# The first load of a one-token decode layer, w_mod, issued as two DMAs: 16 rows, then 112

## The chip, the cores and the metric

The kernel runs on one core of one Trainium2 chip. A core has five instruction engines (TensorE for matrix products, VectorE, ScalarE, GpSimd and SyncE, which here only issues loads) and 16 DMA engines that move data between the chip's large memory and the core's on-chip buffer of 128 partitions. The metric is the device time of one execution in microseconds, as a median over runs.

## The reference, cut to what matters

One token passes through an attention block over a long cache and a gated feed-forward block. A conditioning vector `c` gives six vectors of 640 numbers that scale and shift the layer norms and gate both blocks:

```python
x = A_x
mod = (_silu(c) @ w_mod).reshape(c.shape[0], 6, 1, -1)   # w_mod: 640 x 3840, bf16
sa, ca, ga, sb, cb, gb = (mod[:, 0], ..., mod[:, 5])
h = _layernorm(x) * (1 + ca) + sa
x = x + ga * _A_ref(h, A_k_cache, A_v_cache, A_wq, A_wo)   # 32 heads, 16384 cached keys and values of 128
h = _layernorm(x) * (1 + cb) + sb
x = x + gb * _B_ref(h, B_w_gate, B_w_up, B_w_down)         # silu(h @ w_gate) * (h @ w_up) @ w_down, 1728 wide
```

The two caches are 32 x 16384 x 128 numbers of two bytes each, 134 MB apiece; all weights together are some 22 MB. Every byte is used once.

## The kernel before, in words

All instructions are recorded first as operations with their dependencies, and a small planner then writes each engine's list in the order of recording, with a wait on a semaphore wherever an operation needs one of another engine (`_Plan.emit`, from line 122). A DMA raises the semaphore of its own channel by 16 when it has landed; a waiter waits for the count that the channel has after the DMA it depends on. Every large load is issued by SyncE, so SyncE's list is the order of the stream of loads, and a load that has to wait (for a buffer to come free) holds back every load behind it. The method that issues a load has line 90, so all loads show as L90.

The stream goes: `w_mod` (line 351), `A_wq` (352), the keys of head pair 0 in two halves, the keys of pair 1, the values of pair 0, and then keys and values of the 16 head pairs by turns, then `A_wo`, `B_w_gate`, `B_w_up`, `B_w_down`. Two loads of 1.2 KB, `c` and `A_x`, are issued by ScalarE at the start (354 and 355). The keys have a ring of two buffers, `kring`, and the values one, `vbuf`. `w_mod` is put into the second key buffer and `A_wq` into the value buffer, since both are free at the start.

The loads are laid out so that every partition takes one piece of the source: partition p of `w_mod` holds rows 5p to 5p+4 of the matrix, 5 x 3840 numbers that lie side by side in memory, 38,400 bytes. A row of the load, in this text, is these 38,400 bytes of one partition. A row of `A_wq` is 40,960 bytes, and a row of one pair's keys or values 65,536 bytes (32,768 in the halves of pair 0).

The start of the kernel runs so: `c` and `x` are turned into columns on TensorE (line 378), ScalarE and VectorE compute the silu of `c` and the layer norm of `x`, and when `w_mod` has landed TensorE multiplies (line 438, 40 matmuls in two halves), VectorE picks the diagonal out (446, 451) and makes `h_col` (460). When `A_wq` has landed, TensorE computes the queries (477) and ScalarE spreads them (484). The load of the keys of pair 1 waits for the second half of the `w_mod` product, because it overwrites the buffer of `w_mod`; the load of the values of pair 0 waits for the last query product. From there on VectorE works through the keys of each pair (a product with the query and two or three folding additions, lines 554, 559, 564 in the loop and 570, 576 for the first and last pair), TensorE sums what is left (544, 584), ScalarE takes the exponential, and TensorE multiplies with the values (518). The keys of pair p+1 are loaded when pair p-1 has been summed.

After the last pair come the output projection with `A_wo` (687, 699), the second layer norm, the gate and up products (724), the down product (771) and two small stores.

The lines around the change are these:

```python
wm_v = kb[:, 0:KC * 6 * D].rearrange("p (k n) -> p k n", k=KC)
wm_src = w_mod.rearrange("(p k) n -> p k n", p=128)
d_wm = dma(wm_v, wm_src, "wm", name="dma_wmod")
d_wq = dma(wq_v, wq_src, "wq", name="dma_wq")
```

`d_wm` is used in one place, as a dependency of the two halves of the product with `w_mod`:

```python
o_mod = [op(PE, lambda e, h=h: f_mod(e, h), deps=[d_wm, o_sc], name="mod_mm%d" % h) for h in range(2)]
```

Of the kernel before, what the change touches and what calls it, by code (L numbers as in the profile page):

```python
# [37 lines left out]
class _Plan:  # L38
# [44 lines left out]
    def dma(self, out_ap, in_ap, key, deps=(), name="", eng="sp", noncontig=False):  # L83
        nc = self.nc

        def fn(e, out_ap=out_ap, in_ap=in_ap, noncontig=noncontig):
            if noncontig:
                with nc.allow_non_contiguous_dma(reason="tiny vector layout change"):
                    return e.dma_start(out_ap, in_ap)
            return e.dma_start(out_ap, in_ap)  # L90

        return self.op(eng, fn, deps, name, chan=self.dma_chan(key))
# [126 lines left out]
def build(nc, A_x, A_k, A_v, A_wq, A_wo, B_wg, B_wu, B_wd, c_in, w_mod, out):  # L219
# [23 lines left out]
    with es:  # L243
        block = es.enter_context(nc.Block())
        plan = _Plan(nc, es)
        op, dma = plan.op, plan.dma
# [10 lines left out]
        wm_v = kb[:, 0:KC * 6 * D].rearrange("p (k n) -> p k n", k=KC)  # L257
# [88 lines left out]
        wm_src = w_mod.rearrange("(p k) n -> p k n", p=128)  # L346
# [1 line left out]
        k_src = lambda p: A_k[0, 2 * p:2 * p + 2].rearrange("h (q t) d -> (h q) t d", q=64)  # L348
        v_src = lambda p: A_v[0, 2 * p:2 * p + 2].rearrange("h (q t) d -> (h q) t d", q=64)

        d_wm = dma(wm_v, wm_src, "wm", name="dma_wmod")
        d_wq = dma(wq_v, wq_src, "wq", name="dma_wq")
        op(ACT, lambda e: e.preload_act_table_set("natural_log_exp_and_others"), name="tbl")
        d_c = dma(rows[:, 0, :], c_in, "c", name="dma_c", eng="act")
# [430 lines left out]
def bass_adaLN_cond__gqa_block_cached__swiglu_ffn__decode_kernel(  # L785
    nc: bass.Bass,
    A_x: bass.AP,
    A_k_cache: bass.AP,
    A_v_cache: bass.AP,
    A_wq: bass.AP,  # L790
    A_wo: bass.AP,
    B_x: bass.AP,
    B_w_gate: bass.AP,
    B_w_up: bass.AP,
    B_w_down: bass.AP,
    c: bass.AP,
    w_mod: bass.AP,
    out: bass.AP,
):
    build(nc, A_x, A_k_cache, A_v_cache, A_wq, A_wo, B_w_gate, B_w_up, B_w_down, c, w_mod, out)  # L800
# [28 lines left out]
```

## Time and profile before

| what | value |
|---|---|
| median of 3 runs | 680.17 us (679.9 to 680.23) |
| profiled execution, its own time | 679.98 us |
| its span from the first to the last instruction | 678.2 us |
| busy: TensorE, VectorE, ScalarE | 366.2, 513.0, 46.7 us (54%, 76%, 7% of the span) |
| DMA | 6355 packets, 290.58 MB, mean 428 GB/s over the span |

The profiled execution's time is 1.78 us longer than its span; the difference lies before the first and after the last instruction. Busy time is the sum over an engine's instructions, so an engine that is busy for 76% of the span may still have waited at every step. The chain of waits is read backwards from the last instruction: at each step it names what released it. The start of an instruction and its duration stand in front of each line of the timeline and of the chain. A DMA issue has two times: the short one for which SyncE (SPq) or ScalarE (ACTq) was occupied in issuing it, and the time from issue to landing, which includes waiting behind earlier loads in the same stream.

### The profile page before, as it was taken

Reading aid. Unit: us, or ns where it says so; the run is one execution under the profiler, and the core shown is the slowest. Engines: PE = TensorE matmul, PEld = TensorE weight load, DVE = VectorE, ACT = ScalarE, POOL = GpSimd, SP = SyncE. Lnnn points to the kernel's source line nnn. Section 1 sums busy time; section 2 is a strip of 40 time slices with the busy share of each in tenths; the row PEclk is TensorE's granted clock in tenths of the full one; section 3 lists DMA queues with packets and bytes.
Section 4 is the critical chain, followed back from the end, with each engine's and each line's share of the span. In section 5 each row is a group of like instructions: output and inputs, shape, how many; then the busy total and the mean of one; then the engine's idle time right before and its main releaser. Section 6 shows DMA issues by size and latency. Waiting matters only on the chain.

```text
span 678.2 us, 5410 instructions
## 1 busy us (share of the span) xinstructions
PE 366.2 (54%) x2068; PEld 146.5 (22%) x2069; DVE 513.0 (76%) x185; ACT 46.7 (7%) x147; POOL 0.7 (0%) x6
## 2 busy tenths in 40 slices
PE   2522275755728274664818375572818465471677
PEld 1111122221312122221302122121212222130236
DVE  2189997959596896959597795959699695959812
ACT  1120000100000000000000010000000000000011
POOL 0000000000000000000000000000000000000000
PEclk9675565655657565565757555575756556575765
DMA  9999999999999999999999999999999999999997
GB/s 372 442 459 433 433 433 430 433 430 433 437 430 433 433 433 433 433 437 433 433 433 433 437 433 433 433 433 433 433 433 433 433 433 433 433 437 433 434 402 305
DMA packets 6355, 290.58 MB, mean 428 GB/s; under 512 B 714, under 2 KB 972, under 8 KB 1484
## 3 DMA queue, kind: packets, MB, share of 16 engines
q1 hardware_dynamic: 6340, 290.48, 99.2%
q8 instruction: 5, 0.08, 0.0%
q10 hardware_dynamic: 8, 0.00, 0.0%
q14 instruction: 2, 0.02, 0.0%
HBM read 290.47 MB, written 0.00 MB: 428 GB/s over the span
## 4 chain that ended last, share of the span: by engine, by line
DMA 48%; DVE 28%; issue 13%; PE 11%; DVEq 0%; ACT 0%; SPq 0%
DMA kring<-in_A_k_cache_dram 45%; DVE kring L554 10%; PE psb L544 7%; DVE kring L559 6%; DVE kring L570 4%; DVE kring L576 3%; DMA vbuf<-in_A_wo_dram 3%; DVE kring L564 3%; PE psb L518 1%; PE psb L724 1%; PE psb L687 1%; PE psb L584 1%; PE psb L699 0%; PE psb L771 0%; DVE pm L590 0%
## 5 line engine op out<-in xcount | busy, mean ns | idle before, releaser
L554 DVE TENSOR_TENSOR kring<-kring,qbc 128x16384 bf16<-128x16384 bf16 x28 | 243.2, 8687 | 96.2 <-DMA kring<-in_A_k_cache_dram 96.2
L544 PE MATMUL psb<-kring,ident 128*128 x448 | 197.5, 607 | 119.3 <-DVE kring L564 119.3
L559 DVE TENSOR_TENSOR kring<-kring 128x8192 bf16<-128x8192 bf16 x28 | 123.8, 4420 | 0.5
L544 PEld LDWEIGHTS psb<-kring,ident 128*128 128x128 bf16 x448 | 53.9, 120 | 247.1 <-issue 246.0
L518 PE MATMUL psb<-vbuf,PZ 128*8 128x512 bf16 x960 | 82.6, 520 | 0.0
L594 PE MATMUL psb<-d,bd_f 128*128 128x64 f32 x32 | 11.0, 446 | 122.0 <-ACT d L592 122.0
L564 DVE TENSOR_TENSOR kring<-kring 128x4096 bf16<-128x4096 bf16 x28 | 64.0, 2286 | 0.5
L570 DVE TENSOR_TENSOR kring<-kring,qbc 128x16384 bf16<-128x16384 bf16 x4 | 34.8, 8688 | 23.4 <-DMA kring<-in_A_k_cache_dram 23.4
L518 PEld LDWEIGHTS psb<-vbuf,PZ 128*8 128x8 bf16 x960 | 27.0, 109 | 60.2 <-issue 51.5
L584 PE MATMUL psb<-kring,ident 128*128 128x128 bf16 x64 | 14.5, 392 | 40.3 <-DVE kring L576 40.3
L594 PEld LDWEIGHTS psb<-d,bd_f 128*128 128x128 f32 x32 | 8.0, 311 | 124.1 <-DVE pm L590 114.4
L576 DVE TENSOR_TENSOR kring<-kring 128x8192 bf16<-128x8192 bf16 (+2 forms) x12 | 31.7, 2645 | 0.3
L533 PEld LDWEIGHTS psb<-sel,acc_sb 128*128 128x128 f32 x128 | 28.5, 311 | 8.4 <-issue 4.3
L533 PE MATMUL psb<-sel,acc_sb 128*128 128x2 f32 x128 | 25.6, 322 | 1.4 <-ACT acc_sb L524 1.4
L524 ACT ACTIVATE acc_sb<-psb 128x512 f32<-128x512 f32 x16 | 9.6, 597 | 212.0 <-PE psb L518 212.0
L602 ACT ACTIVATE PZ<-psb,nb 64x256 bf16<-64x256 f32 x32 | 15.0, 469 | 64.8 <-DVE nb L598 64.6
L584 PEld LDWEIGHTS psb<-kring,ident 128*128 128x128 bf16 x64 | 7.4, 122 | 46.7 <-DVE kring L576 41.6
L592 ACT ACTIVATE d<-negid,pm 128x64 f32<-128x64 f32 x16 | 5.6, 348 | 153.9 <-DVE pm L590 153.9
L477 PE MATMUL psb<-vbuf,h_col 128*128 128x512 bf16 x39 | 11.2, 461 | 8.3 <-DMA vbuf<-in_A_wq_dram 8.3
L537 ACT ACTIVATE OT_sb<-psb 128x2 f32 (+1 forms) x16 | 2.8, 172 | 151.3 <-PE psb L533 151.3
L590 DVE TENSOR_REDUCE pm<-psb 128x1 f32<-128x256 f32 x16 | 6.7, 418 | 3.7 <-PE psb L584 3.7
L477 PEld LDWEIGHTS psb<-vbuf,h_col 128*128 128x128 bf16 x40 | 4.3, 116 | 15.6 <-DMA vbuf<-in_A_wq_dram 8.8
(104 smaller groups left out, 80.4 us busy)
## 6 DMA issues: line engine op xcount, KB each, us to landing
kring<-in_A_k_cache_dram SPq DMA_DIRECT2D x2, 4096.0 KB, 40.3
vbuf<-in_A_wq_dram SPq DMA_DIRECT2D x1, 5120.0 KB, 25.9
kring<-in_w_mod_dram SPq DMA_DIRECT2D x1, 4800.0 KB, 14.2
vbuf<-in_A_wo_dram SPq DMA_DIRECT2D x1, 4480.0 KB, 23.0
kring<-in_B_w_gate_dram SPq DMA_DIRECT2D x1, 2160.0 KB, 18.7
kring<-in_B_w_up_dram SPq DMA_DIRECT2D x1, 2160.0 KB, 23.5
kring<-in_B_w_down_dram SPq DMA_DIRECT2D x3, 640.0 KB, 25.7
vbuf<-in_A_wo_dram SPq DMA_DIRECT2D x1, 640.0 KB, 24.2
```

The costliest lines, as they stand in the source:

```text
L477: last = e.matmul(q_ps[b][:, 0:512], lhsT=h_col[:, k:k + 1].broadcast_to([128, 128]), rhs=wq_v[:, k, g * 512:(g + 1) * 512], start=(k == 0 ...
L518: last = e.matmul(acc_ps[32 * s:32 * s + 8, :], lhsT=PZ[:, j, :], rhs=v_at(p)[:, 4 * j:4 * j + 4, :].rearrange("p t d -> p (t d)"), start= ...
L533: last = e.matmul(OT_ps[:, 0:2], lhsT=acc_sb[:, 128 * i:128 * (i + 1)], rhs=sel[:, i:8:4], start=(i == 0), stop=(i == 3))
L544: last = e.matmul(S_ps[:, 0:T2], lhsT=ident[:], rhs=kring[:, bass.ds(plan.slot(p), 1), :, d].rearrange("p o t -> p (o t)"), start=(d == 0) ...
L554: return e.tensor_tensor(out=kv4, in0=kv4, in1=q4, op=ALU.mult)
L559: o_f = op(DVE, lambda e: e.tensor_tensor(out=kv4[:, :, 0], in0=kv4[:, :, 0], in1=kv4[:, :, 1], op=ALU.add), deps=[o_m], name="fold%d_%d" ...
L564: return op(DVE, lambda e: e.tensor_tensor(out=lo[:, :, 0:QR], in0=lo[:, :, 0:QR], in1=lo[:, :, QR:QW], op=ALU.add), deps=[o_f], name="fol ...
L570: o = op(DVE, lambda e: e.tensor_tensor(out=kv, in0=kv, in1=qbc[:, p, :].unsqueeze(1).broadcast_to([128, KCUT[c + 1] - KCUT[c], 128]), op= ...
L576: o = op(DVE, lambda e, w=w: e.tensor_tensor(out=kv[:, :, 0:w], in0=kv[:, :, 0:w], in1=kv[:, :, w:2 * w], op=ALU.add), deps=[o], name="fol ...
L584: last = e.matmul(S_ps[:, KCUT[c]:KCUT[c + 1]], lhsT=ident[:], rhs=kring[:, p % 2, KCUT[c]:KCUT[c + 1], d], start=(d == 0), stop=(d == 15))
L594: o_mx[p] = op(PE, lambda e: e.matmul(mx_ps[:, 0:64], lhsT=bd_f[:], rhs=d2[:], start=True, stop=True), deps=[o_d2, o_bd1, o_bd2, o_nb[p - ...
L602: o_exp[p] = op(ACT, lambda e, half=half, ps=ps: e.activation(out=PZ[ps, :, 4 * half:4 * half + 4], in_=S_ps[ps, 0:T2].rearrange("p (c i) ...
```

## The change

The load of `w_mod` becomes two loads on the same channel: partitions 0 to 15 first, then partitions 16 to 127. The variable on which the product waits is that of the second load, and since both count on one channel, its count is reached when both have landed. Source, destination and bytes are the same; `A_wq` and all later loads are issued as before, behind them.

```diff
-        d_wm = dma(wm_v, wm_src, "wm", name="dma_wmod")
+
+        dma(wm_v[0:16], wm_src[0:16], "wm", name="dma_wmod0")
+        d_wm = dma(wm_v[16:128], wm_src[16:128], "wm", name="dma_wmod1")
         d_wq = dma(wq_v, wq_src, "wq", name="dma_wq")
```

## The prediction

> **What bounds the kernel now.** I read the DMA queues first, then the busy time by stretches, then the chain of waits, then the first microseconds of the timeline. The page's third part and the stretches of time (columns: stretch, length, busy time and instructions of each engine, TensorE's granted clock, share of the 16 DMA engines, GB/s) say:
>
> ```profile
> q1 hardware_dynamic: 6340, 290.48, 99.2%
> ```
>
> ```profile
> 0.00:15.00 15.00, 1.70 (x14) 1.48 (x14) 3.83 (x21) 2.49 (x9) 0.70 (x6) 1.00 0.91 372
> 15.00:37.00 22.00, 13.59 (x72) 5.21 (x74) 3.49 (x9) 4.37 (x12) 0.00 (x0) 0.77 1.00 432
> ...
> 150.00:300.00 150.00, 86.87 (x423) 31.87 (x423) 119.54 (x33) 8.79 (x27) 0.00 (x0) 0.57 1.00 433
> ...
> 450.00:600.00 150.00, 83.02 (x417) 31.00 (x415) 122.58 (x32) 8.96 (x28) 0.00 (x0) 0.57 1.00 433
> ```
>
> The reader is to see that SyncE's queue keeps the 16 DMA engines occupied from the first load to nearly the last, at one rate, 433 GB/s, which is 27.06 GB/s for each engine. VectorE, the busiest of the others, has 122.58 us of work in a stretch of 150. So the stream is the bound. The chain in order of time agrees, at its start and its end:
>
> ```profile
> 0.80 0.40 SPq L90
> ...
> 1.26 0.41 SPq L90
> ...
> 1.73 35.15 DMA kring<-in_A_k_cache_dram
> 36.89 8.70 DVE kring L570
> ...
> 570.12 38.73 DMA kring<-in_A_k_cache_dram
> ...
> 635.21 22.98 DMA vbuf<-in_A_wo_dram
> ```
>
> It begins with the loads; VectorE starts on the first keys at 36.89, the moment they land. A pair's keys and values are 16.78 MB, 38.75 us at 433 GB/s: the 38.73 us that a key load needs from issue to landing is nothing but the stream in front of it and itself. What is lost or won at the head of the stream is therefore passed on one for one: the first keys land later by it, VectorE's run from 36.89 shifts, the later loads queue behind, and no stretch from 15 us to 600 us in these rows has idle DMA time that could take it back. What counts is the slowest of the 16 engines, since a load has landed when all have finished.
>
> **The change, part by part.** Issues and landings at the head, from the timeline and from the page's last part (KB each, microseconds to landing):
>
> ```profile
> 0.80 0.40 SPq L90 DMA_DIRECT2D kring<-in_w_mod_dram  x1
> ...
> 1.26 0.41 SPq L90 DMA_DIRECT2D vbuf<-in_A_wq_dram  x1
> ...
> 1.40 0.22 ACTq L90 DMA_DIRECT2D qbc<-in_A_x_dram  x1
> ```
>
> ```profile
> vbuf<-in_A_wq_dram SPq DMA_DIRECT2D x1, 5120.0 KB, 25.9
> kring<-in_w_mod_dram SPq DMA_DIRECT2D x1, 4800.0 KB, 14.2
> ```
>
> A 128-row load costs SyncE 0.40 us, a 1-row load 0.22 us. The 4800 KB of w_mod are 4.915 MB, 11.35 us at 433 GB/s; so 14.2 - 11.35 = 2.85 us of the landing are issue and start. A row of 38,400 bytes takes an engine 38,400 / 27.06 = 1.42 us, and eight rows to an engine make the 11.36.
>
> *An earlier start.* If the time of an issue grows with its rows, 16 rows cost SyncE little more than the 0.22 us of one row, and the first row starts up to 0.18 us sooner. The bounds are 0 and, if the slow start of the first rows went too, 1.5 us: in the packet records the first rows took 1.43 to 2.78 us instead of 1.42, so the worst engine lost 1.36 us, and 1.36 + 0.18 = 1.54. I take 0.2 us, by the issue rows, because the first reads of the kernel stay first reads in either form.
>
> *One more issue on SyncE.* It costs 0.22 to 0.41 us, and what is queued behind it is the load of A_wq and the keys of pair 0. Their rows are needed only when w_mod is through, 14.2 us after its issue, and the A_wq issue now ends at 1.67: the cover is over 10 us, so nothing. The second part must be issued before an engine has finished its first row: 0.40 us against 1.42, so nothing either; without this cover each engine would idle for at most the 0.40. The 16 additional completion records took 9 ns each in the packet records, one to an engine: nothing. TensorE's wait on w_mod stays one wait.
>
> *The shape of the two loads.* Here is the large term. Every load over 1.2 KB in this profile covers all 128 partitions, and the 16 engines then move 433 GB/s. The change for the first time has 16 engines write 16 neighbouring partitions at once. No row shows whether the partitions take that. The lower end is 1.42 us for the 16 rows, if each partition takes a full engine's rate whatever its neighbours get. The upper end is 16 x 1.42 = 22.7 us, if neighbours have one entrance that passes one engine's rate. Between ends so far apart I take the geometric middle, 5.7 us, which is four engines to an entrance (4 x 1.42 = 5.68), or 16 partitions behind four of 16 entrances. The whole rate, 16 times one engine's, is 16 such entrances with eight partitions each.
>
> The sum under that: all engines are held for 5.68 us instead of 1.42, +4.26. But the loss is larger. During the 5.68 us four entrances have passed four rows each, as many as in the old form, and twelve have passed none; each of the twelve still has eight rows to pass, 8 x 1.42 = 11.36, so w_mod cannot be in before 5.68 + 11.36 = 17.04 us of moving, 5.68 more than now. And the second load gives seven consecutive rows to each engine (112 / 16), whose blocks no longer fit groups of eight partitions or fewer: neighbouring engines meet at an entrance. If that costs the slowest engine as much again as the first row did, another 4.26, it is 5.68 + 4.26 = 9.94. Between 5.68 and 9.94 I take the middle, 7.81; the engines can evade each other partly, since they soon run out of step. After w_mod each engine has its own share of a 128-row load again, and the delay is carried along.
>
> [...]
>
> **Sum.** -0.2 + 0 + 0 + 7.8 = +7.6 us on the profiled execution's 679.98, 687.6; the median of the runs lies 0.19 above that execution, so 687.8 for the median. With the ends, -0.2 + 4.26 and -0.2 + 9.94, the likeliest case's own range is 684.2 to 689.9. What is late next is the product with w_mod (now from 15.07 us), the queries, and the first key product at 36.89, each by the same 7.6 us; none of them overtakes another, since A_wq and the keys are later by as much.
>
> **The rivals.** *The partitions take it (0.24).* Four engines on neighbouring partitions do not hinder each other. For it: an engine's rate, 27.06 GB/s, may be the engine's own limit and not that of an entrance; the profile cannot tell. Against: that 16 times 27.06 is reached only where loads cover 128 partitions. It decides at the 16 rows' time: at 1.42 us a row the delay is nothing and the 0.18 us of the shorter issue are left: 680.0 for the median, not slower.
>
> *The change does not do what it says (0.06).* The 16 rows go to the few engines that serve these partitions in a 128-row load, four rows each. The second load then gives these engines four rows fewer, every engine still has its eight rows, and the stream ends as before: 680.2.
>
> *A clearly earlier start (0.02).* All of the 1.54 us above is won: 678.6. Against it: the loads of c and x, which reach TensorE only at 7.35 us, show that first reads are slow in any form.
>
> *Rows dealt in turn (0.08).* The second load gives each engine every sixteenth row, so that the 16 engines stay on 16 neighbours through all eight rows: 8 x 4.26 = 34 us, 714. For it, nothing in the rows; against, that engines out of step would spread.
>
> **How the numbers follow.** The forecast has the remaining 0.60, because 433 GB/s at exactly 16 equal rates fits shared entrances as well as engine limits, and because most divisions of 16 rows over entrances other than a perfect one cost more than the small gain at the start. About 0.2%, 1.36 us here, is what a measurement of this kernel can tell from no change. Faster by more: 0.02. Within: 0.24 + 0.06 = 0.30. Slower: 0.60 + 0.08 = 0.68. The range must take in the first two rivals to leave out no more than 0.2: from 679.6, 0.4 under the first rival, to 691.0, 1.1 above the likeliest case's end; it leaves out the last two rivals, 0.10.
>
> **What would show it.** Right: w_mod lands not at 15.0 us but at 21 to 25 (its second load), the stretch from 0 to 15 us falls well under 372 GB/s, the first keys are met at 41 to 47 us instead of 36.89, every later key load still takes 38.7 us, and the rows from 150 us on are the same. Step by step: the first issue shows its 0.2 us in SyncE's row, the start in the first landing, the second load's collision in how far w_mod's landing exceeds 15.0 + 4.26. Wrong: w_mod lands at 15 us as before (first two rivals), or the delay is there at 37 us but smaller at the end, which would mean a reserve in the stream that these rows do not show.

## The result, and the profile after

The changed kernel takes 691.07 us (median of 6 runs, 690.69 to 691.39) against 680.12 us (6 runs, 679.9 to 680.34): 10.95 us more, a ratio of 1.0161 with a 95% interval of 1.0148 to 1.0174. The span of its profiled execution is 689.6 us.

The first SyncE queue and the stretches of time show where it went (columns as in the prediction; the last two are the share of the DMA engines and GB/s):

```profile
q1 hardware_dynamic: 6356, 290.48, 99.1%
```

```profile
0.00:15.00 15.00, 1.71 (x14) 1.48 (x14) 3.83 (x21) 2.49 (x9) 0.70 (x6) 1.00 0.95 205
15.00:37.00 22.00, 3.53 (x40) 1.32 (x40) 3.37 (x8) 0.30 (x1) 0.00 (x0) 0.89 0.98 343
150.00:300.00 150.00, 83.48 (x418) 31.09 (x416) 122.18 (x32) 8.54 (x28) 0.00 (x0) 0.57 1.00 434
450.00:600.00 150.00, 81.08 (x409) 30.66 (x402) 119.26 (x32) 8.96 (x28) 0.00 (x0) 0.58 1.00 433
```

The bytes are the same, and the DMA engines are as occupied as before: 0.95 and 0.98 in the first two stretches. But they move 205 and 343 GB/s there, not 372 and 432. An occupied DMA engine is not a DMA engine at its rate: by the packet records (each row's transfer with its start and duration) a row of w_mod took an engine 1.69 to 4.95 us here, against 1.42 before once the start was over, and all of that counts as busy. From 150 us on the rate is as before, 433 to 434 GB/s.

The issues of w_mod (shortest, median and longest issue in ns, and the times to landing), and the landings of the loads in the page's form:

```profile
L90 SPq DMA_DIRECT2D kring<-in_w_mod_dram x2: 388/396/404, 0.8 to 1.2; - x2
...
DMA to landing us min/median/max: 7.3/16.1/24.8
```

```profile
vbuf<-in_A_wq_dram SPq DMA_DIRECT2D x1, 5120.0 KB, 36.3
...
kring<-in_w_mod_dram SPq DMA_DIRECT2D x1, 4200.0 KB, 24.8
...
kring<-in_w_mod_dram SPq DMA_DIRECT2D x1, 600.0 KB, 7.3
```

The 600 KB of the 16 rows need 7.3 us to land, and the 4200 KB 24.8 us from their issue at 1.2; the whole 4800 KB had landed after 14.2. The timeline and the chain show that the delay is then carried along:

```profile
26.13 3.53 PE L440 MATMUL psb<-kring,silu_c 128*32 128x480 bf16 x40 [15.12 <-DMA kring<-in_w_mod_dram]
...
47.72 8.69 DVE L572 TENSOR_TENSOR kring<-kring,qbc 128x16384 bf16<-128x16384 bf16 x1 [15.81 <-DMA kring<-in_A_k_cache_dram]
```

```profile
2.24 45.46 DMA kring<-in_A_k_cache_dram
...
580.14 38.72 DMA kring<-in_A_k_cache_dram
```

The product with w_mod starts at 26.13 instead of 15.08, the first keys are met at 47.72 instead of 36.89, 10.83 later, and a key load in the loop still takes 38.7 us. The wait for the last key load of the chain starts 10.02 later than before (580.14 against 570.12), and the two profiled executions differ by 11.31 at the end (691.29 against 679.98). So what is added at the head reaches the end, give or take about a microsecond on the way.

### The profile page after: what moved, and what is told of

Read it like the earlier page. It is cut to its first block, busy times and chain, and to the rows that moved or that the text cites. A ratio compares the mean times of both kernels' runs of the same rounds, so it can differ in the third digit from the quotient of the medians.

```text
span 689.6 us, 5412 instructions
## 1 busy us (share of the span) xinstructions
PE 359.4 (52%) x2069; PEld 144.1 (21%) x2069; DVE 513.0 (74%) x185; ACT 46.7 (7%) x147; POOL 0.7 (0%) x6
## 4 chain that ended last, share of the span: by engine, by line
DMA 49%; DVE 29%; issue 12%; PE 8%; SPq 0%; DVEq 0%
DMA kring<-in_A_k_cache_dram 45%; DVE kring L556 10%; PE psb L546 7%; DVE kring L561 6%; DVE kring L572 5%; DVE kring L578 5%; DMA kring<-in_B_w_down_dram 4%; DVE kring L566 3%; PE psb L586 1%; SPq L90 0%; DVE pm L592 0%; DVE nb L600 0%; PE psb L773 0%; DVEq L191 0%; DVEq L556 0%
## 5 line engine op out<-in xcount | busy, mean ns | idle before, releaser
L520 PE MATMUL psb<-vbuf,PZ 128*8 128x512 bf16 x960 | 78.7, 500 | 0.0
L440 PE MATMUL psb<-kring,silu_c 128*32 128x480 bf16 x40 | 3.5, 526 | 15.1 <-DMA kring<-in_w_mod_dram 15.1
## 6 DMA issues: line engine op xcount, KB each, us to landing
kring<-in_w_mod_dram SPq DMA_DIRECT2D x1, 4200.0 KB, 24.8
```

The costliest lines, as they stand in the source:

```text
L520: last = e.matmul(acc_ps[32 * s:32 * s + 8, :], lhsT=PZ[:, j, :], rhs=v_at(p)[:, 4 * j:4 * j + 4, :].rearrange("p t d -> p (t d)"), start= ...
```

## The experiments

The theory of place says: a load is slow when the 16 DMA engines write to partitions that lie close together at one time. Its picture, that such partitions share an entrance of the on-chip buffer and the engines then write to few entrances at once, is an assumption: no trace shows an entrance, and the runs can show only whether the place of the rows sets their time. The rivals are the theory of number (a second load, its issue and its records cost), the theory of memory reads (the rows that are read together collide in the large memory), the theory of the cold start (the 16 rows are slow because they are the first reads), and the theory that 112, not being a power of two, is handled worse.

**Two loads by columns.**

```diff
-        d_wm = dma(wm_v, wm_src, "wm", name="dma_wmod")
+        dma(wm_v[:, 0:1], wm_src[:, 0:1], "wm", name="dma_wmod0")
+        d_wm = dma(wm_v[:, 1:KC], wm_src[:, 1:KC], "wm", name="dma_wmod1")
```

> w_mod is again loaded in two, but by columns: both loads cover all 128 partitions, the first with 7,680 bytes of each, the second with 30,720. Theory of place (partitions that lie close together share an entrance of the on-chip buffer, so what counts is how many different entrances the 16 DMA engines write to at once): no crowding, so the first keys are met at 36.9 us as before and the time is 680.1, within 0.5 us. Theory of number (the second load, its issue and its completion records are the cost): as the changed kernel, w_mod late by about 10 us and 691. Theory of a better start: up to 1.5 us less, 678.6.

Measured: 679.96 us against 680.15, ratio 0.9998 (0.9989 to 1.0007). The first keys and the last key load of the chain:

```profile
36.33 8.69 DVE L571 TENSOR_TENSOR kring<-kring,qbc 128x16384 bf16<-128x16384 bf16 x1 [16.02 <-DMA kring<-in_A_k_cache_dram]
```

```profile
570.21 38.72 DMA kring<-in_A_k_cache_dram
```

Two loads cost nothing that can be measured, so the theory of number falls. They gain nothing either: in this trace the first keys are met 0.56 us earlier than before, but the wait for the last key load starts at 570.21, before at 570.12. A lead of that size was not passed on.

**A probe of 16 rows, in three forms.** The first:

```diff
+        p_src = w_mod.rearrange("(p k) n -> p (k n)", p=128)
+        dma(kb[0:16, 19200:32000], p_src[0:16, 0:12800], "wm", name="probe")
         d_wm = dma(wm_v, wm_src, "wm", name="dma_wmod")
```

> w_mod is loaded whole as in the kernel before. Ahead of it goes a probe that nothing uses: 16 rows of 25,600 bytes into partitions 0 to 15, to bytes that are free; the product with w_mod waits for it as well. At 27.06 GB/s a row is 0.95 us. Theory of place, four engines to an entrance: 4 x 0.95 = 3.8 us, so the first keys come at 40.7 and the total is 683.9. If the partitions were not shared: 0.95 us, 681.1. Theory of memory reads (the rows read together collide in the large memory): the same time as the next probe, which reads the same rows.

The second writes to `kb[0:112:7, ...]` from the same rows:

> The same probe, the same 16 source rows, but written to every seventh partition, 0 to 105. [...] Theory of place: between 0.95 and 1.9 us instead of 3.8, so 681.1 to 682.0 and the first keys at 37.8 to 38.8. Theory of memory reads, and theory of number: the same time as the probe into partitions 0 to 15, whatever that is.

The third writes to `kb[0:16, ...]` from `p_src[0:112:7, ...]`:

> The same probe into partitions 0 to 15, but read from every seventh source row. Theory of place: the same as the probe into partitions 0 to 15 from neighbouring rows, 683.9 if that is right. Theory of memory reads: different from that probe by a microsecond or more.

Measured, on one chip beside 680.15: neighbours 682.85 (ratio 1.0041, 1.0025 to 1.0056), spread 681.51 (1.002, 1.0011 to 1.003), neighbours from spread rows 683.22 (1.0045, 1.003 to 1.006). The issue lines of the first and of the second (KB, microseconds to landing) show the same bytes:

```profile
kring<-in_w_mod_dram SPq DMA_DIRECT2D x1, 400.0 KB, 5.5
```

```profile
kring<-in_w_mod_dram SPq DMA_DIRECT2D x1, 400.0 KB, 4.1
```

For 16 rows, where they are written decides: from the same source rows the spread probe costs half, +1.36 against +2.70, within the 0.95 to 1.9 expected for it. The 0.95 is one row's time and the 1.9 that of two; no run shows how many rows meet. Where they are read from matters little: the third probe lies 0.37 us above the first, with intervals that overlap, and an effect of that size is not excluded. So the theory of memory reads falls as the main cause, and the theory of place holds in this, that neighbours cost more than spread rows; that entrances are the reason is not shown. Its number, 3.8, was a good microsecond too high. The packet records show why: the start of the kernel before is itself uneven, its first 16 rows are done 2.97 us after the first one starts, 1.55 more than a row's 1.42. That loss runs beside the crowding and is mostly not added to it: in the table further down, 16 neighbours take 5.35 us at the first step and 5.29 at each later one.

**Probes of 112 and 128 rows.** As above with `[16:128]` and `[0:128]` on both sides.

> w_mod is loaded whole; ahead of it goes a probe of 112 rows of 25,600 bytes into partitions 16 to 127, to bytes that are free. It is the changed kernel's second load alone, without the 16 rows. If seven rows to an engine went at full rate: 7 x 0.95 = 6.6 us, 686.8. [...] Theory of the cold start (only the first 16 rows hurt, and what follows them): close to 686.8.

> Control for the probes: 128 rows of 25,600 bytes over all partitions ahead of the whole w_mod load, 16 rows more than the probe of 112 rows. All theories that blame the place: eight rows at full rate, 8 x 0.95 = 7.6 us, 687.7, which is less than the 690.7 of the 112 rows although more is loaded. If extra loads at the head cost by themselves, more than that.

Measured: 690.73 with 112 rows (ratio 1.0156, 1.0139 to 1.0173), beside 680.15; 687.54 with 128 rows (1.0109, 1.0092 to 1.0126), beside 680.11. Landings:

```profile
kring<-in_w_mod_dram SPq DMA_DIRECT2D x1, 2800.0 KB, 13.4
```

```profile
kring<-in_w_mod_dram SPq DMA_DIRECT2D x1, 3200.0 KB, 10.1
```

More bytes in less time. The 128 rows cost 7.43 us, what their bytes cost (7.6); the 112 rows cost 10.58, 4.0 more than theirs (6.6). At the changed kernel's rate of 246 GB/s they would cost 7 x 0.95 x 433 / 246 = 11.7, an estimate. The second load of the change is slow by itself, without the 16 rows ahead of it.

**Two halves.** `wm_v[0:64]` and `wm_v[64:128]`.

> w_mod in two loads of 64 rows, partitions 0 to 63 and 64 to 127, four rows to each engine. [...] Theory that the cost in the changed kernel comes from 112 not being a power of two (and 16 being few): none of it here, 680.2.

Measured: 692.14 us, ratio 1.0175 (1.0158 to 1.0192), 12.0 more. 64 is a power of two, and the split costs all the same. In the packet records the median row takes 3.00 us at six of the eight steps, 2.1 times 1.42 (2.67 at the first and 2.78 at the fifth). Four steps of 3.00 us for the 2,457,600 bytes of 64 rows are 205 GB/s.

**The 112 rows dealt out by hand.** Two kernels, each with the 16 rows first and then seven loads of 16 rows:

```diff
-        d_wm = dma(wm_v[16:128], wm_src[16:128], "wm", name="dma_wmod1")
+        for j in range(7):
+            d_wm = dma(wm_v[16 + j:128:7], wm_src[16 + j:128:7], "wm", name="dma_wmod%d" % (j + 1))
```

> The first 16 rows as in the changed kernel, then the other 112 as seven loads of 16 rows, one to each engine: load j takes partitions 16 + j, 23 + j, ... 121 + j. If the single load of 112 rows gives each engine seven consecutive rows, this is the same work in the same steps, and the time is that of the changed kernel, 691.1 within 1 us. If what costs is the number of loads, six more loads must show: six times 10 us by that theory's reading of the change, or at least six issues of 0.4 us, 693.5. If 112 as a number is at fault, the second part goes at full rate: 682 to 684.

```diff
-        d_wm = dma(wm_v[16:128], wm_src[16:128], "wm", name="dma_wmod1")
+        for j in range(16, 128, 16):
+            d_wm = dma(wm_v[j:j + 16], wm_src[j:j + 16], "wm", name="dma_wmod%d" % j)
```

> w_mod as eight loads of 16 neighbouring rows, partitions 0 to 15, 16 to 31 and so on. Theory of place: at every step 16 engines write to 16 neighbours, four to an entrance: 8 x 5.68 = 45.4 us of moving, 34 us more, less about 1 us of the start's spread: 712 to 714. If neighbours share less than that, by the first rows of the changed kernel (median 4.36 us, of which some 0.6 us are the start), 8 x 3.7 = 30 us, 18 more: 698. Theory of number: as the kernel with seven loads behind the first 16 rows.

Measured, beside 680.15: every seventh row 691.23 us (ratio 1.016, 1.0143 to 1.0177), 16 neighbours at a time 711.06 us (1.0455, 1.0438 to 1.0473). Eight loads in both, and 20 us between them, so the number of loads does not set the time; 711.06 is a microsecond under the range worked out. That 112 as a number is at fault falls as well, since seven loads of 16 rows take the time of one load of 112. The stretches of the changed kernel, of the kernel with every seventh row, and of the one with neighbours:

```profile
10.00:15.00 5.00, 0.59 (x2) 0.50 (x2) 1.73 (x10) 0.67 (x4) 0.00 (x0) 1.00 0.78 246
15.00:20.00 5.00, 0.00 (x0) 0.00 (x0) 0.00 (x0) 0.00 (x0) 0.00 (x0) 1.00 1.02 246
20.00:25.00 5.00, 0.00 (x0) 0.00 (x0) 0.00 (x0) 0.00 (x0) 0.00 (x0) 1.00 0.95 254
```

```profile
10.00:15.00 5.00, 0.59 (x2) 0.50 (x2) 1.70 (x9) 0.44 (x3) 0.00 (x0) 1.00 0.81 238
15.00:20.00 5.00, 0.00 (x0) 0.00 (x0) 0.00 (x0) 0.00 (x0) 0.00 (x0) 1.00 1.07 253
20.00:25.00 5.00, 0.00 (x0) 0.00 (x0) 0.00 (x0) 0.00 (x0) 0.00 (x0) 1.00 0.89 238
```

```profile
10.00:15.00 5.00, 0.58 (x2) 0.50 (x2) 1.80 (x10) 0.67 (x4) 0.00 (x0) 1.00 1.06 123
15.00:20.00 5.00, 0.00 (x0) 0.00 (x0) 0.00 (x0) 0.00 (x0) 0.00 (x0) 1.00 1.06 123
20.00:25.00 5.00, 0.00 (x0) 0.00 (x0) 0.00 (x0) 0.00 (x0) 0.00 (x0) 1.00 1.07 123
```

The DMA engines are occupied throughout in all three: these rows count a packet in the stretch in which it starts, which gives 0.78 to 1.07, and counted by its own time the share is 1.00 to 1.01 in each stretch. A finer view, from the packet records: the time after the start of the first row at which 16, 32, ... 128 rows of w_mod were done, in us.

| kernel | 16 | 32 | 48 | 64 | 80 | 96 | 112 | 128 |
|---|---|---|---|---|---|---|---|---|
| before | 2.97 | 4.39 | 5.81 | 7.22 | 8.64 | 10.06 | 11.47 | 12.89 |
| changed | 5.20 | 8.03 | 10.73 | 13.17 | 15.24 | 17.85 | 20.44 | 23.16 |
| 16, then every seventh row | 5.19 | 8.07 | 10.71 | 13.24 | 15.45 | 18.04 | 20.74 | 23.33 |
| 16 neighbours at a time | 5.35 | 10.66 | 15.95 | 21.24 | 26.53 | 31.82 | 37.11 | 42.41 |

The second and third line agree within 0.3 us at every step. So the one load of 112 rows behaves as one that gives each engine seven consecutive rows, and not as rows dealt in turn. The last line gives the price of 16 neighbours once the start is over: 5.29 us a step, 3.73 times 1.42, or 614,400 bytes / 5.29 us = 116 GB/s. That is 4.3 times an engine's 27.06, so 16 neighbouring partitions take what about four engines deliver.

**The other order.** The 112 rows first, then the 16, with `d_wm` the second.

> The same two loads in the other order: the 112 rows first, then the 16. Theory of place: the same rows collide in the same steps, seven steps at 246 GB/s and one at 116 GB/s, so about the changed kernel's 691.1, between 690 and 692.5; the last row must now show 5.3 us a step. Theory that the 16 rows hurt because they are the first reads of the kernel: nearly no cost of theirs here, 688 or less.

Measured: 691.15 us, ratio 1.0162 (1.0145 to 1.0179). The order does not matter for the total. In the packet records the 112th row is done at 17.65 us against 11.47 before, 6.18 more, and the 16 rows, now last, end 5.35 us after it, 3.93 more than a row's 1.42. The theory of the cold start falls. But how the loss divides does depend on the order: the load that comes first hides the uneven start.

**Another load.** A_wq in 16 and 112 rows, w_mod whole.

> w_mod is loaded whole; the second load of the kernel, A_wq, is split into 16 and 112 rows in its place. Its rows are 40,960 bytes, 1.51 us. Theory of place: the 16 rows take 5.29 x 40,960 / 38,400 = 5.64 us instead of 1.51, which is 4.1 more, without the start's 1.5 us to hide in; the 112 rows cost 8.05 x 1.067 = 8.6 more; together 12.7, less what the steps overlap: 691.5 to 693. Theory of the cold start: no more than 0.5 us, 680.6.

Measured: 693.16 us, ratio 1.0195 (1.0178 to 1.0212), 13.05 more, 0.35 above the sum of 12.7 made from the steps of w_mod and just over the range. By the packet records A_wq lands 12.91 us later than before, so nearly all of it is there at the head. The parts are less well met than their sum: its 16th row is done 5.28 later, worked out 4.1, and the other 112 add 7.63, worked out 8.6. That the sum came out so close is in part luck.

## Why the prediction was wrong

The direction was right, and for the 16 rows nearly the factor: four times a row's time was assumed, and a step of 16 neighbours took 3.73 times. That few entrances for neighbouring partitions are the mechanism is not shown. The size was not right: 7.6 us were forecast, 10.95 came, just over the range and 1.2 over the end that the likeliest case was given for itself. The step that failed is the cost of the second load.

- *What bounds the kernel, and that a delay at the head is passed on whole:* right within about a microsecond. In the profiled executions the delay is 10.83 us at the first keys, 10.02 at the last key load of the chain and 11.31 at the end; the medians give 10.95. The lead of 0.56 us with two loads by columns was lost on the way.
- *An earlier start, -0.2:* wrong, and small. The two issues took 388 and 404 ns, so 16 rows cost SyncE as much as 112; the row of 0.22 us is that of a 1.2 KB load on ScalarE's queue, where the other load of that size, c, took 0.53 to issue. The first row of w_mod starts at 1.83 us before and after. Two loads by columns, with the first keys 0.56 us earlier in their trace, changed the median by -0.19 us, not told from nothing.
- *The further issue and its records, 0:* right; two loads by columns and eight loads against two show it.
- *The 16 rows, four engines to an entrance, +4.26:* no run shows an entrance, nor that there are 16 with eight partitions each: these were assumptions, and the four the middle between two ends. What the runs showed in their place is 5.29 us for a step of 16 neighbours, 116 GB/s. So the factor was nearly right, 3.73, which is 3.87 us a step over a row's 1.42. But at the head it added only 5.20 - 2.97 = 2.23, because the uneven start, 1.55 us, runs beside it. So this term was 2.0 too high.
- *The second load:* this is the term that failed. The prediction let it cost between 1.42 (5.68 - 4.26, which rests on the assumed entrances) and 5.68 us, "as much again as the first row did, another 4.26" being the upper end, and took the middle, 3.55, because "the engines can evade each other partly, since they soon run out of step". Measured: from the 16th to the 128th row 17.96 us against 9.92, 8.04 more, and another 0.4 at the first rows of A_wq. The loss comes at every one of the seven steps, which take 2.07 to 2.83 us instead of 1.42, where the prediction priced one such loss for the whole load. With the 112 rows first it is 6.18, still more than the upper end. So this term was 4.5 too low; the two together are 10.3 where 7.8 stood, and the forecast came as near as it did because the two errors partly cancelled.

The rivals: that the partitions take it is excluded by the probes. That the rows go to the few engines of a 128-row load is excluded as well, since that would have cost nothing. Rows dealt in turn are not what the load does, but the kernel that does it by hand took 711.1, near the 714 worked out for it. A clearly earlier start did not come. The argument against it misread a row, though: in the packet records the 1.2 KB of x took 0.06 us, at 5.45 us, so x was late because its transfer started late and not because the read was slow.

What stays open is why the 112 rows cost as much as they do. In the packet records of the changed kernel no row of that load took less than 1.69 us, and the median row of a step took 1.9 to 3.1, against 1.42 before: all the rows are slow, and not only a few that meet. The runs show that it is so, with one load or seven; they do not show which of the engines hinder each other, or where. Nor do they separate, for the 112 rows, where the rows are written from where they are read, as the three probes do for 16. That place is the cause is shown for the 16 rows, and argued for the 112.

## What to carry to other kernels

In a kernel that is bound by its loads, split a load by bytes within the partitions, not by partitions: here a column split was free and every row split cost 11 to 31 us. Look at what the 16 engines write at one time, and not only at what a load covers in all: partitions 16 to 127 were loaded at about 246 GB/s, where 128 partitions get 433. A count of assumed entrances pointed the right way here but gave too little, 7.8 us where 10.3 came, so the time of the rows has to be measured. A share of DMA busy time near 1 says nothing of the rate: between 15 and 20 us it was 1.02 at 246 GB/s in the changed kernel and 1.06 at 123 with 16 neighbours at a time, and 1.00 at 433 later in the stream. A gain at the start of the first load was at most some tenths of a microsecond here, 0.56 at the first keys with two loads by columns, and was not passed on, so a change that aims at it has to cost nothing elsewhere.

## What the runs showed that was not expected

- A crowded first step hides the uneven start: of the 3.87 us that a step of 16 neighbours costs over a row's 1.42, 2.23 showed at the head of the changed kernel.
- The starts of the engines at A_wq lie 0.95 us apart before, 0.31 behind the probe of 16 neighbours and 0.40 behind the two loads by columns, one trace each; so a more even start is not the crowding's doing alone.
- 64 partitions in two loads cost more than 16 and 112: 692.14 against 691.07. Nearly every step of theirs is a double one (3.00 us).
- The time of an issue on SyncE does not follow the rows: 0.39 us for 16 rows and 0.40 for 112 in the changed kernel, 0.55 and 0.58 for 64 rows each in the two halves.
